# A new head for an interleaved attention and gMLP kernel: tokens, wq, wk, wv, with later background work queued behind its step

## The chip, the core and the metric

The kernel runs on one core of one Trainium2 chip. The metric is device time in microseconds (us), the median of several executions of the whole program. The core has a matrix engine (TensorE, PE in the profile), VectorE (DVE), ScalarE (ACT), GpSimd (POOL) and SyncE (SP), which here issues all transfers. Each engine runs its own instructions in order and waits for others by semaphores.

## What is computed

Four layers over x of 2048 tokens by 640: attention with a compressive memory, gMLP, the same attention again, the same gMLP again, with the same weights. Float32 results are kept by splitting each operand into a high and a low float16 part and summing three products. The reference, cut:

```python
def _A_ref(x, wq, wk, wv, wo, beta):            # H = 32 heads of Dh = 20, N = 4 segments of L = 512
    q, k, v = heads(x @ wq), heads(x @ wk), heads(x @ wv)
    for s in range(N):
        p = softmax(qs @ ks.T * scale + causal_mask)
        a_dot = p @ vs
        a_mem = (phi(qs) @ M) / (phi(qs) @ z + 1e-6)
        outs.append(g * a_mem + (1 - g) * a_dot)         # g = sigmoid(beta)
        M, z = M + phi(ks).T @ vs, z + sum(phi(ks))
    return concat(outs) @ wo
def _B_ref(x, w_in, w_sp, b_sp, w_out):
    z = gelu(x @ w_in)                                    # 2 x 864 columns
    g = w_sp @ layernorm(z[..., Fh:]) + b_sp[:, None]
    return (z[..., :Fh] * g) @ w_out
x = x + _A_ref(layernorm(x), ...)
x = x + _B_ref(layernorm(x), ...)
x = x + _A_ref(layernorm(x), ...)
x = x + _B_ref(layernorm(x), ...)
```

## The kernel before

Each of the two rounds has an attention phase (`phase1a`, class `Attention`), a phase with the output projection's rest and w_in (`phase1b`), and a phase with w_sp and w_out (`phase2`).

**Weights.** A weight is scaled by a power of two and split. `pow2_scales` finds the scale: largest magnitudes per partition, a PE transpose (tile `wtp`), a maximum over it (`wmx`), a diagonal (`wdg`), a PE product that spreads it to all partitions (`wbc`), and five small DVE steps to `pw` and its inverse `iv`. `split_scaled` makes the high part on ACT and the low part on DVE. `prologue` (L117) loads wv, wq and wk, in this order, five tiles of 128x640 each (`wst`), takes their maxima (`wamk`), scales and splits them, and computes small scalars. The maxima of wo, w_in and w_out come from `other_scales` (L168): 32 tiles `wmst` through a pool of two buffers, one DVE reduction each into `wap`, and one scale chain for all four.

**Attention.** A segment has 512 tokens, four tiles. `prep(t)` loads a tile of x, takes layernorm statistics (`lnst`), normalises, splits (high on ACT, low on POOL, tile `xnhl`) and transposes by a transfer into `xt`. `value(t)` makes v of a tile (`vps`), `unit(s, m)` one of five groups of 128 rows of q and k (`qps`, `kps`), which `out` splits (`qhl`, `khl`), stores to DRAM (`st`) and, for k, turns into features (`phl`, `pk`) for the memory update. In the first layer the head of the phase is: prep of tiles 0 to 3, values of 0 to 3, units 0 and 1. In the second layer `early` does this inside `phase2` of the round before.

**The loop.** `run` goes through 64 pairs of heads (16 in each segment), three steps for each pair, from step -10 (`LEAD`) on. A step issues scores: `mp` for the row maxima (`mx`, DVE) of the pair two ahead, `es` for this pair's exponentials (`P`, ACT, L865). Around them come casts (`PH` on ACT, `PL` on POOL), the products with v (`pv`), row maxima sent to the rows of `qk` (`mr`), and `fetch` of the next pair's q and k. Four streams are merged into it by due step, in `until`: `fills` (prep and loads for later values and projections, 11 and 3.5 steps ahead), `background` (`other_scales`, then load and split of wo and of half of w_in, paced in steps), `dense` (units, values and projections), `reads` (the memory's reads).

**Order.** The written order holds for PE alone. On the other engines and their queues the order is planned at build time by readiness and by priority, so an instruction that is ready early may be issued far ahead of where it is written. PSUM tiles `dn` (for `vps`, `qps`, `kps`) have two buffers, `mp` and `es` one each.

Of the kernel before, what the change touches and what calls it, by code (L numbers as in the profile page):

```python
# [47 lines left out]
def pow2_scales(g, pool, psum, tag, am, c0, n):  # L48

# [6 lines left out]
    nc.vector.tensor_scalar(dg[:n, :n], g.ident[:n, :n], mx[:n], None, ALU.mult)  # L56
    bc = psum.tile([128, 128], F32, tag=tag, name="wbc")
# [7 lines left out]
    nc.vector.tensor_scalar(iv, iv, WTOP, None, ALU.mult)  # L65


def split_scaled(g, h, l, st, c):

    nc = g.nc  # L70
    iv = g.iv[:st.shape[0], c:c + 1]
    nc.scalar.activation(h, st, AF.Identity, scale=iv)
    nc.vector.scalar_tensor_tensor(l, st, iv, h, ALU.mult, ALU.subtract)
# [43 lines left out]
def prologue(g, ctx, wv, wq, wk, wo, w_in, w_out):  # L117

    nc, tc = g.nc, g.tc
    wp = ctx.enter_context(tc.tile_pool(name="wqkv", bufs=1))  # L120
    g.w = {}
# [4 lines left out]
    nc.vector.memset(g.wap, 0.0)  # L126
    g.wam = wp.tile([128, 8], F32, name="wam")
    with tc.tile_pool(name="wpro", bufs=1, side="right", reuse_waits="tile") as p, \
            tc.tile_pool(name="wpp", bufs=1, space=PSUM, reuse_waits="tile") as pp:
        am = p.tile([128, 4, KD], F32, name="wamk")  # L130
        st = {}
        for i, (nm, dram) in enumerate((("v", wv), ("q", wq), ("k", wk))):
            st[nm] = p.tile([128, KD, D], F32, name="wst" + nm)
            for k in range(KD):
                nc.sync.dma_start(st[nm][:, k, :], dram[k * 128:(k + 1) * 128, :])
        for i, nm in enumerate("vqk"):
            for k in range(KD):
                nc.vector.tensor_reduce(am[:, i, k:k + 1], st[nm][:, k], AX.X, ALU.max, apply_absolute_value=True)
            nc.vector.tensor_reduce(g.wam[:, i:i + 1], am[:, i], AX.X, ALU.max)
            pow2_scales(g, p, pp, "wsc", g.wam, i, 1)  # L140
            h = wp.tile([128, KD, D], F16, name=f"w{nm}h")
            l = wp.tile([128, KD, D], F16, name=f"w{nm}l")
            for k in range(KD):
                split_scaled(g, h[:, k], l[:, k], st[nm][:, k], i)
            g.w[nm] = (h, l)

    pq, pk = g.pw[:, 1:2], g.pw[:, 2:3]
    s = lambda n: g.sc[:, n:n + 1]
    g.esc, g.rq, g.rk, g.gq, g.gk, g.sig, g.epsd, g.yw, g.zi, g.pofs = s(0), s(1), s(2), s(3), s(4), s(5), s(6), s(7), (s(8), s(9)), s(10)
    nc.vector.tensor_scalar(g.esc, pq, pk, SCALE / 16, ALU.mult, ALU.mult)  # L150
# [9 lines left out]
    nc.vector.tensor_scalar(g.rk, pk, 2.0 ** -24, None, ALU.mult)  # L160
    nc.vector.tensor_scalar(g.gq, g.iv[:, 1:2], XS, None, ALU.mult)
    nc.vector.tensor_scalar(g.gk, g.iv[:, 2:3], XS, None, ALU.mult)
    nc.vector.tensor_scalar(g.sig, pk, 1.0, 2.0 ** -20, ALU.min, ALU.mult)
# [4 lines left out]
def other_scales(g, stage, pool, psum, tag):  # L168
# [3 lines left out]
    for i, w in enumerate((g.wo, *g.wi, g.wu)):  # L172
        width = D if w.cols == D else w.cols // 2
        j = 0
        for k in range(w.nk):
            n = min(128, w.dram.shape[0] - 128 * k)
            for c in range(0, w.cols, width):
                t = stage.tile([128, D], F32, tag="bg", name="wmst")[:n, :width]
# [346 lines left out]
class Attention:  # L525
# [9 lines left out]
    def __init__(self, g, x, o_d, x1_d, kept):  # L535
# [11 lines left out]
        self.now, self.later, self.rd = None, {}, set()  # L547

    def post(self, k, f, free=False):
# [52 lines left out]

    def prep(self, t):
# [16 lines left out]
        return stats, norm  # L620

    def value(self, t):
# [5 lines left out]
        for n in range(2):  # L628
# [8 lines left out]
            def out(ps=ps.rearrange("p (h d) -> p h d", d=DH), v=self.vs[s % 2][:, t % 4, n * 16:(n + 1) * 16, :]):  # L637
                nc.scalar.mul(v[:, :, 0:DH], ps, QS)
                nc.vector.scalar_tensor_tensor(v[:, :, DH + 1:], ps, QS, v[:, :, 0:DH], ALU.mult, ALU.subtract)
# [39 lines left out]
    def unit(self, s, m):  # L679
# [3 lines left out]
        for nm in ("q", "k"):  # L683
            wh, wl = g.w[nm]
            ps = self.pd.tile([128, L], F32, tag="dn", name=f"{nm}ps")
# [118 lines left out]
    def fetch(self, n):  # L804
# [3 lines left out]
        for h in range(2):  # L808
            c = 40 * (n % 16) + 20 * h
            self.nc.sync.dma_start(self.qk[n % self.NQK][64 * h:64 * h + 60], self.st[n // 16 % 2][c:c + 20].rearrange("p l i c -> (p l) i c"))  # L810
# [19 lines left out]
    def scores(self, n, c):  # L830
# [30 lines left out]
        if 0 <= n < self.N:  # L861
# [3 lines left out]
            nc.scalar.activation(P[:, :, 512 * c:512 * c + ew], es[:, :, :ew], AF.Exp, scale=g.esc)  # L865
            if c == 2:
                self.last = n
        if 0 <= m < self.N:
            if c == 0:
                self.mx[m] = self.pl2.tile([128, 2, 4], F32, tag="mx", name="mx")  # L870
            for i, o, w in red:
                nc.vector.tensor_reduce(self.mx[m][:, :, i], mp[:, :, o:o + w], AX.X, ALU.max)  # L872
# [13 lines left out]
    def maxes(self, n):  # L886
# [7 lines left out]
        for i in range(2):  # L894
            nc.sync.dma_start(self.qk[n % self.NQK][60 + i:125 + i:64, 0].rearrange("h (t c) -> h t c", t=4), mr[:, i])
# [48 lines left out]
    def run(self, nseg=NSEG):  # L944
# [82 lines left out]
        def background():  # L1027

            g = self.g
# [10 lines left out]
        if self.stacked < 0:  # L1040
            for t in range(0, 4, 2):
                for f in zip(self.prep(t), self.prep(t + 1)):
                    f[0]()
                    f[1]()
                if t == 0:
                    self.start()
            for i in range(4, 8):
                self.early(i)
        else:
            self.start()  # L1050
# [109 lines left out]
```

## Time and profile before

| | |
|---|---|
| median of 3 runs | 2444.76 us (2442.37 to 2446.39) |
| profiled execution, its own time | 2440.32 us |
| its span, first to last instruction | 2438.6 us |
| mean granted TensorE clock | 0.975 |
| PE busy | 2218.2 us (91%) |
| DVE busy | 1434.3 us (59%) |
| ACT busy | 1133.7 us (46%) |
| POOL busy | 936.1 us (38%) |

The lines below are of that one execution. A timeline line gives the start in us from the span's start, the duration in us, the engine, the line of the kernel, the operation, the tile written and those read, and the count; in square brackets the time that the engine stood idle before it and what ended the wait. A line of a group gives count, busy us and mean ns, then idle time before its members and its releasers. A line of the stretches gives the length, each engine's busy us with its instructions, the granted clock, the share of the DMA engines and GB/s. Busy PE time is modelled and no measure of PE at its peak.

### The profile page before, as it was taken

Reading aid. Unit: us, or ns where it says so; the run is one execution under the profiler, and the core shown is the slowest. Engines: PE = TensorE matmul, PEld = TensorE weight load, DVE = VectorE, ACT = ScalarE, POOL = GpSimd, SP = SyncE. Lnnn points to the kernel's source line nnn. Section 1 sums busy time; section 2 is a strip of 40 time slices with the busy share of each in tenths; the row PEclk is TensorE's granted clock in tenths of the full one; section 3 lists DMA queues with packets and bytes.
Section 4 is the critical chain, followed back from the end, with each engine's and each line's share of the span. In section 5 each row is a group of like instructions: output and inputs, shape, how many; then the busy total and the mean of one; then the engine's idle time right before and its main releaser. Section 6 shows DMA issues by size and latency. Waiting matters only on the chain.

```text
span 2438.6 us, 50718 instructions
## 1 busy us (share of the span) xinstructions
PE 2218.2 (91%) x20682; PEld 1319.0 (54%) x20682; DVE 1434.3 (59%) x2766; ACT 1133.7 (46%) x1388; POOL 936.1 (38%) x728
## 2 busy tenths in 40 slices
PE   3698789999899989999997989999988997999998
PEld 2355455666555545555554556565654554555554
DVE  8668878777654555444326777877764452454441
ACT  3278777777632222212124988777762221121110
POOL 3168678888610100000002988887871010000000
PEclk9899999999999999999999999999998998999999
DMA  6824634344553488766445253443455345665762
GB/s 196 214 57 109 162 115 122 93 117 133 146 143 107 113 223 206 171 157 164 114 127 133 77 119 88 113 109 93 123 160 124 88 108 165 163 169 155 175 127 58
DMA packets 502505, 325.00 MB, mean 133 GB/s; under 512 B 408512, under 2 KB 443456, under 8 KB 497152
## 3 DMA queue, kind: packets, MB, share of 16 engines
q1 hardware_dynamic: 502272, 321.76, 51.4%
q8 instruction: 162, 2.65, 0.5%
q14 instruction: 71, 0.58, 0.1%
HBM read 148.25 MB, written 85.34 MB: 96 GB/s over the span
## 4 chain that ended last, share of the span: by engine, by line
PE 60%; DVE 11%; DMA 11%; ACT 7%; issue 5%; POOL 3%; SPq 3%; ACTq 0%; DVEq 0%; POOLq 0%
PE gp L380 16%; PE zp L295 14%; PE cyp L409 6%; PE pv L909 3%; PE yps L666 3%; PE kps L690 3%; DMA wr<-in_B_w_sp_dram 3%; PE vps L633 3%; PE mp L856 3%; PE qps L690 3%; ACT PH L882 2%; ACT P L865 2%; PE es L856 2%; POOL PL L883 2%; DVE mx L872 2%
## 5 line engine op out<-in xcount | busy, mean ns | idle before, releaser
L883 POOL TENSOR_TENSOR PL<-P,PH 128x1280 f16<-128x1280 f32 x248 | 649.8, 2621 | 155.2 <-ACT PH L882 145.6
L380 PE MATMUL gp<-zh,wt 128*128 128x432 f16 x2048 | 466.5, 348 | 24.0 <-DMA wt<-wn 24.0
L872 DVE TENSOR_REDUCE mx<-mp 128x2 f32<-128x1024 f32 (+3 forms) x512 | 409.4, 818 | 108.1 <-PE mp L828 106.2
L380 PEld LDWEIGHTS <-wt 128*128 128x128 f16 x3072 | 301.8, 98 | 286.5 <-DMA wt<-wn 25.7
L865 ACT ACTIVATE P<-es,sc 128x1024 f32<-128x1024 f32 (+1 forms) x384 | 370.3, 964 | 128.5 <-PE es L828 122.6
L882 ACT CAST PH<-P 128x1280 f16<-128x1280 f32 x256 | 320.5, 1253 | 19.0 <-PE pv L909 12.0
L295 PEld LDWEIGHTS <-th 128*128 128x128 f16 x1920 | 188.9, 99 | 177.8 <-issue 11.7
L380 PE MATMUL gp<-zl,wt 128*128 128x432 f16 x1024 | 272.8, 348 | 0.0
L395 POOL MEMSET un<- 128x64 f16 x32 | 4.8, 151 | 675.7 <-DMA ut<-un 588.9
L205 POOL TENSOR_TENSOR lnrs<-lnve,mhalf 128x1 f32<-128x1 f32 x96 | 58.6, 618 | 484.6 <-DVE lnve L204 459.6
L856 PEld LDWEIGHTS <-qk 60*128 60x128 f16 (+1 forms) x2048 | 93.0, 94 | 222.2 <-issue 155.1
L357 DVE TENSOR_REDUCE am<-wr 128x1 f32<-128x2048 f32 x32 | 73.2, 2286 | 214.7 <-DMA wr<-in_B_w_sp_dram 214.6
L383 ACT ACTIVATE u<-gp,bsp,un 128x864 f32<-128x864 f32 x32 | 34.2, 1068 | 355.5 <-PE gp L380 355.5
L409 PE MATMUL cyp<-wuh,ut 128*128 128x320 f16 (+1 forms) x896 | 166.8, 303 | 15.4 <-DMA ut<-un 15.4
L633 PE MATMUL vps<-wvh,xt 128*128 128x320 f16 x640 | 156.3, 310 | 22.5 <-DMA xt<-xnhl 13.8
L856 PE MATMUL es<-qk 64*128 64x512 f16 (+3 forms) x1024 | 135.2, 299 | 41.6 <-ACT P L865 26.9
L409 PEld LDWEIGHTS <-ut 128*128 128x128 f16 (+1 forms) x1344 | 132.6, 99 | 73.7 <-DMA ut<-un 17.4
L909 PE MATMUL pv<-vs,PL 128*128 128x41 f16 x2560 | 163.8, 181 | 7.3 <-POOL PL L883 4.5
L909 PE MATMUL pv<-vs,PH 128*128 128x41 f16 x2560 | 167.8, 182 | 1.2 <-DVE ab L925 1.2
L828 PEld LDWEIGHTS <-big 64*128 64x128 f16 x3072 | 141.7, 95 | 49.8 <-issue 3.1
L856 PE MATMUL mp<-qk 60*128 60x512 f16 (+3 forms) x1024 | 137.8, 306 | 31.1 <-DVE mx L872 28.6
L367 ACT ACTIVATE wn<-wr,ivw 128x1024 f16<-128x1024 f32 x64 | 71.9, 1144 | 194.6 <-DVE ivw L362 111.1
(182 smaller groups left out, 4138.5 us busy)
## 6 DMA issues: line engine op xcount, KB each, us to landing
wr<-in_B_w_sp_dram SPq DMA_DIRECT2D x32, 1024.0 KB
qk<-st SPq DMA_DIRECT2D x256, 120.0 KB
x<-x SPq DMA_DIRECT2D x56, 320.0 KB
z<-z SPq DMA_DIRECT2D x32, 432.0 KB
cz<-z SPq DMA_DIRECT2D x32, 432.0 KB
xt<-in_A_x_dram SPq DMA_DIRECT2D x32, 320.0 KB
st<-qhl SPq DMA_DIRECT2D x40, 256.0 KB
st<-khl SPq DMA_DIRECT2D x40, 256.0 KB
```

Source lines behind the costliest of these rows:

```text
L295: nc.tensor.matmul(zp[:, n, :FHH], a[:, k, :], b[:, k, c:c + FHH], start=(k == 0 and j == 0), stop=(k == KD - 1 and j == 2))
L380: nc.tensor.matmul(gp[:, n, :FHH], wt[:, k // 8, a, k % 8, :], b[:, k, n * FHH:(n + 1) * FHH], start=(k == 0 and j == 0), stop=(k == NT - ...
L409: nc.tensor.matmul(yp[:, n, :320], a[:kn[k], k, :], b[:kn[k], k, n * 320:(n + 1) * 320], start=(k == 0 and j == 0), stop=(k == KO - 1 and ...
L633: nc.tensor.matmul(ps, a[:, k, c], b[:, k, n * 320:(n + 1) * 320], start=(i == 0), stop=(i == 14))
L690: nc.tensor.matmul(ps, a[:, k, c], b[:, k, :], start=(i == 0), stop=(i == 14))
L828: nc.tensor.matmul(out, g.big[r, 64 - 64 * s:192 - 64 * s], mk, start=False, stop=s == 1, skip_group_check=True)
L856: nc.tensor.matmul(out[:, h, o:o + w], a[r, ac], b[r, bc], start=o == 0, stop=False, skip_group_check=True)
L865: nc.scalar.activation(P[:, :, 512 * c:512 * c + ew], es[:, :, :ew], AF.Exp, scale=g.esc)
L872: nc.vector.tensor_reduce(self.mx[m][:, :, i], mp[:, :, o:o + w], AX.X, ALU.max)
L882: nc.scalar.copy(PH, P[:, h])
L883: (nc.gpsimd if h == 0 or n < self.N - self.TAIL else nc.vector).tensor_tensor(PL, P[:, h], PH, ALU.subtract)
L909: nc.tensor.matmul(pv[:, i, h, :], x[:, c:c + 128], v[:, j, h0 + h, :], start=(j == 0 and x is PH), stop=(j == i and x is PL), skip_group_ ...
```

## The change

- `prologue` becomes `attn_weights` (tiles only) and `attn_scalars`; the work moves into `Attention.head`, which replaces the first layer's preps, values and early units. Loads: four tiles of x at once, wq, wk; wv is queued behind the four transposes of x. Then statistics of all four tiles, one power on POOL for all, four transposes; q's maxima, scale, splits; k's maxima queued behind q's second split; q of units 0 and 1; k's scale, splits; v's maxima behind k's second split; the scalars; k of units 0 and 1; v's scale and splits; the values. q and k of the head use the PSUM tiles of `es` and `mp`.
- `last_of` keeps the last traced exponential or value copy on ACT, row maximum or value copy on DVE, and fetch, maxima or weight transfer on SP. Under `hold()`, whatever is traced on these engines gets an order edge behind them: no wait for their end, only a later place in the queue. `until` runs `fills` and `background` under it, `prep` its statistics and norm, in both layers.
- `background` starts at step -8 and paces the 32 maxima at 0.75 step instead of from step 6 at 1.2. The scale chain is cut in two (`pow2_max`, `pow2_spread`), at steps 51 and 53, with the last maximum at 50. The transfer of b_sp moves behind it. The pools for wo and w_in are opened after the head.

```diff
+def pow2_max(g, pool, psum, tag, am, c0, n):      # pow2_scales up to wdg
+def pow2_spread(g, psum, tag, dg, c0, n):         # the rest of it
...
-    yield False
+    yield 50
     nc.vector.tensor_reduce(g.wam[:, 3:7], g.wap, AX.X, ALU.max)
-    pow2_scales(g, pool, psum, tag, g.wam, 3, 4)
+    yield 51
+    dg = pow2_max(g, pool, psum, tag, g.wam, 3, 4)
+    yield 53
+    pow2_spread(g, psum, tag, dg, 3, 4)
...
+    def hold(self):
+        held = ExitStack()
+        for i in self.last_of.values():
+            held.enter_context(self.tc.issue_after(i))
+        return held
...
+    def head(self):
...
+            for t in range(4):
+                nc.sync.dma_start(xs[:, t], self.x[t])
...
+            def largest(nm, behind):
+                a = p.tile([128, KD], F32, tag="wamk" + nm, name="wamk")
+                with tc.issue_after(behind):
+                    for k in range(KD):
+                        nc.vector.tensor_reduce(a[:, k:k + 1], st[nm][:, k], AX.X, ALU.max, apply_absolute_value=True)
+                i = WNAMES.index(nm)
+                return nc.vector.tensor_reduce(g.wam[:, i:i + 1], a, AX.X, ALU.max).ins
...
+            load("q")
+            load("k")
...
+            for t in range(4):
+                for i in range(2):
+                    nc.vector.bn_stats(sx[:, t, i, :], xs[:, t, i * 320:(i + 1) * 320])
+                nc.vector.bn_aggr(mv[:, t], sx[:, t])
+            nc.vector.tensor_scalar(rs, mv[:, :, 1], EPS, XS ** -2, ALU.add, ALU.mult)
+            nc.gpsimd.tensor_tensor(rs, rs, g.mhalf.to_broadcast((128, 4)), ALU.pow)
+            for t in range(4):
+                i = nc.vector.tensor_scalar(xs[:, t], xs[:, t], mv[:, t, 0:1], rs[:, t:t + 1], ALU.subtract, ALU.mult)
+                nc.scalar.copy(hl[:, t, 0], xs[:, t])
+            for t in (2, 0, 3, 1):
+                (nc.gpsimd if t > 1 else nc.vector).tensor_tensor(hl[:, t, 1], xs[:, t], hl[:, t, 0], ALU.subtract)
+            for t in (0, 1, 2, 3):
+                o = self.xt[0][:, :, :, t * 128:(t + 1) * 128]
+                last = nc.sync.dma_start(o.rearrange("p i k c -> p (i k) c"), hl[:, t].rearrange("p i c -> p (i c)"), transpose=True).ins
+            with tc.issue_after(last):
+                load("v")
+            qp = self.pe.tile([128, 2, 512], F32, tag="es", name="qp")
+            kp = self.px.tile([128, 2, 512], F32, tag="mp", name="kp")
+            largest("q", i.ins)
+            scale("q")
+            i = split("q")
+            largest("k", i[1])
+            units("q", 0, qp)
+            scale("k")
+            units("q", 1, qp)
+            i = split("k")
+            largest("v", i[1])
+            with tc.issue_after(i[-1]):
+                attn_scalars(g)
+            units("k", 0, kp)
+            scale("v")
+            units("k", 1, kp)
+            split("v")
+            for t in range(4):
+                for _ in self.value(t):
+                    pass
+                if t == 0:
+                    with self.hold():
+                        self.start()
...
-        return stats, norm
+        return lambda: held(stats), lambda: held(norm)
...
-            yield 6
+            yield -8
             if not g.wo.made:
-                for i, _ in enumerate(other_scales(g, self.bg, self.pl1, self.pm, "ms")):
-                    yield 6 + 1.2 * i if _ else 53
+                nc.vector.memset(g.wap, 0.0)
+                for i, _ in enumerate(other_scales(g, self, self.pl1, self.pm, "ms")):
+                    yield -8 + 0.75 * i if _ is True else _
+                nc.sync.dma_start(g.bsp, self.b_sp.rearrange("(t p) -> p t", p=128))
...
-                e[0] = next(e[2], None)
+                with self.hold() if e[1] < 2 else ExitStack():
+                    e[0] = next(e[2], None)
```

More of the change, by code (lines that the diff above doesn't have):

```diff
@@ L1040, in run @@
         if self.stacked < 0:
[L1041 to L1048, printed above, removed]
+            self.head()
         else:
             self.start()
+        g = self.g
+        g.top = [self.top.enter_context(g.tc.tile_pool(name=n, bufs=1, side="right", reuse_waits="tile")) for n in ("topi", "topo")][::-1]
         streams = [[next(it), i, it] for i, it in enumerate((fills(), background(), dense(), reads()))]
```

108 lines of the change are left out of this document (60 added, 48 removed).

## The prediction

> **What bounds the kernel now.** I read the table of stretches first, for where TensorE (PE) is not full; then VectorE's (DVE's) groups up to the first exponential; then the timeline of that stretch, and last the same landmarks in the second attention layer, which runs the same loop without a head.
>
> ```profile
> core 0: us, PE busy (x) PEld busy (x) DVE busy (x) ACT busy (x) POOL busy (x), PEclk, DMA share, GB/s
> 0.00:133.00 133.00, 73.73 (x408) 39.41 (x409) 95.17 (x216) 37.33 (x62) 27.05 (x48) 0.91 0.72 193
> 133.00:185.00 52.00, 46.92 (x738) 30.30 (x737) 37.61 (x74) 45.77 (x59) 41.24 (x23) 1.00 0.25 62
> ```
> ```profile
> 5.36 0.82 DVE L138 TENSOR_REDUCE wamk<-wstv 128x1 f32<-128x640 f32 x1
> ...
> 9.17 0.81 DVE L138 TENSOR_REDUCE wamk<-wstv 128x1 f32<-128x640 f32 x1
> ...
> 10.02 0.16 DVE L139 TENSOR_REDUCE wam<-wamk 128x1 f32<-128x5 f32 x1
> ...
> 15.18 0.14 DVE L65 TENSOR_SCALAR iv<-iv 128x1 f32<-128x1 f32 x1
> ...
> 32.78 1.46 SPq L219 DMA_TRANSPOSE xt<-xnhl  x1
> ...
> 36.33 0.45 PE L633 MATMUL vps<-wvh,xt 128*128 128x320 f16 x1 [9.19 <-DMA xt<-xnhl]
> ...
> 56.18 0.45 PE L633 MATMUL vps<-wvh,xt 128*128 128x320 f16 x1 [4.64 <-DMA xt<-xnhl]
> ...
> 67.23 0.59 PE L690 MATMUL qps<-xt,wqh 128*128 128x512 f16 x2
> ...
> 88.20 0.59 PE L690 MATMUL qps<-xt,wqh 128*128 128x512 f16 x2
> ...
> 110.75 1.01 PE L690 MATMUL kps<-xt,wkh 128*128 128x512 f16 x2 [9.52 <-DVE phl L724]
> ...
> 132.79 1.12 ACT L865 ACTIVATE P<-es,sc 128x1024 f32<-128x1024 f32 x1
> ...
> 184.77 1.11 ACT L865 ACTIVATE P<-es,sc 128x1024 f32<-128x1024 f32 x1
> ```
> PE does 73.7 us of work in the first 133 us. Its first real matmul comes at 36.3 because it waits for a transposed tile of x. The head (values of four tiles, q and k of units 0 and 1) ends where unit 2 of segment 0 begins, at 88.2. The first exponential of the loop, step 0, comes at 132.8, that of step 24 (pair 8) at 184.8: 2.17 us a step. From step 0 on the loop is dense: of the next 52 us ScalarE (ACT) works 45.8 and PE 46.9. So what a change of the head is worth is how much earlier step 0 comes, less what it pushes into the loop.
>
> In the head the busy engine is DVE, 95.2 of 133 us:
>
> ```profile
> L181 DVE TENSOR_REDUCE wap<-wmst 128x1 f32<-128x432 f32 (+1 forms) x31 | 20.4, 666 | 10.4 <-DMA wmst<-in_B_w_out_dram 7.9 <-DMA wmst<-in_B_w_in_dram 2.4
> L202 DVE BATCH_NORM_STATS2 lnst<-xt 128x6 f32<-128x320 f32 x20 | 8.8, 479 | 8.1 <-DMA xt<-in_A_x_dram 8.1
> ...
> L616 DVE TENSOR_SCALAR xt<-xt,lnmv,lnrs 128x640 f32<-128x640 f32 x10 | 6.1, 609 | 3.6 <-POOL lnrs L205 3.6
> ...
> L73 DVE SCALAR_TENSOR_TENSOR wkl<-wstk,iv,wkh 128x640 f16<-128x640 f32 x5 | 4.6, 951 | 0.0
> ...
> L138 DVE TENSOR_REDUCE wamk<-wstq 128x1 f32<-128x640 f32 x5 | 4.0, 804 | 0.0
> ```
> Two things here are not needed before step 0: the 31 maxima of the other weights (wap, 20.4 us) and the layernorms of six tiles of segment 1 and later (20 statistics stand for ten tiles, four are the head's). They sit between the steps that PE waits for.
>
> **The change, part by part.** *Loads.* x goes first, then wq, wk. Today's first tiles become usable between 5.36 and 9.17, four intervals, so 0.95 us per 320 KB. The four tiles of x are then there by 5.4 + 3 x 0.95 = 8.2, wq by 13.0, wk by 17.8. wv is queued behind the four transposes; it is used after 40, so this costs nothing unless it lands some 15 us late.
>
> *x.* After the last tile: two statistics (0.96), about 1.1 for aggregate, power and the waits between (an estimate, not a row of its own), four subtractions at 0.61: normalised at 12.7.
>
> ```profile
> L218 POOL TENSOR_TENSOR xnhl<-xt,xnhl 128x640 f16<-128x640 f32 x8 | 11.5, 1444 | 26.3 <-ACT xnhl L217 26.3
> ```
> Low parts of two tiles on POOL end near 13.4 + 2 x 1.44 = 16.3; a transpose is usable 3.55 us after its issue (32.78 to 36.33), so x is transposed by about 21. It is not what PE waits for: that is q.
>
> *The weights on DVE, one after the other.* Largest of q, 5 x 0.80, plus two low parts of x (at most 1.44 each, taken as 0.85): 18.4. The chain from the maximum to the scale took 5.2 us for wv (10.02 to 15.32) with other reductions between its steps; alone I take 4, bounds 3 and 5.2: 22.4. Splits, 5 x 0.95: 27.2. Then the largest of k (4.0), its chain (4), its splits (4.75): 39.9. The same for v: 52.7. PE's instructions are in written order, so it stands at each chain's transpose until the maximum is there; q0, q1, k0, k1 fit between. Head work on DVE that is not in this line (the halves of q and k, the key features, the scalars, some 9 us) mostly falls into the three chains' gaps; I add 2. The first value tile goes with the splits; for the other three, two tiles took 67.23 - 56.18 = 11.05 us today, 5.5 each: 54.7 + 16.5 = **71.2** for the end of the head against 88.2. Bounds: 64 (chains of 3, none of the other DVE work exposed, value tiles 0.8 shorter without today's waits between them, an estimate) and 82 (chains of 5.2, all 9 us of other DVE work exposed).
>
> [...]
>
> ```profile
> 40.00:60.00 20.00, 12.74 (x65) 7.63 (x64) 14.49 (x32) 6.98 (x13) 7.40 (x8) 0.83 0.61 157
> ```
> ```profile
> 83.69 1.01 PE L690 MATMUL kps<-xt,wkh 128*128 128x512 f16 x2 [6.58 <-DVE phl L724]
> ```
> After a wait of 6.58 us two matmuls took 1.01 us, against 0.59 at 88.20, and where PE waited often the granted clock was 0.83. Three islands with eight slow matmuls each, 0.21 us more apiece, are 5 us if all is exposed; I take nothing, since DVE paces q0 and k0, and keep the 5 inside the upper bound. [...]
>
> *From the end of the head to step 0.* Today 132.79 - 88.20 = 44.6. The second layer has no maxima here:
>
> ```profile
> 1280.52 0.60 PE L690 MATMUL qps<-xt,wqh 128*128 128x512 f16 x2
> ...
> 1297.80 1.01 PE L690 MATMUL kps<-xt,wkh 128*128 128x512 f16 x2 [7.77 <-DVE phl L724]
> ...
> 1322.32 1.12 ACT L865 ACTIVATE P<-es,sc 128x1024 f32<-128x1024 f32 x1
> ```
> It takes 41.8 there, with the same stall of unit 3's k on the features of the k before it. So this stretch hardly depends on the maxima: 43, bounds 39 and 47. Step 0 then comes at 114.2, **18.6 earlier** (bounds 4 and 30).
>
> *The maxima in the loop.* 32 of them at 0.75 step each from step -8: 11 fall before step 0, 21 x 0.67 = 14 us after. DVE is idle 52 - 37.6 = 14.4 us in the first 52 us of the loop, where ACT sets the pace. Free if all fit, 14 if none does; they sit between mp and its maximum, on a single buffer, so I take **5 lost**.
>
> *From step 51 on.*
>
> ```profile
> 251.01 1.11 ACT L865 ACTIVATE P<-es,sc 128x1024 f32<-128x1024 f32 x1 [0.88 <-PE es L828]
> ...
> 261.37 1.55 ACT L72 ACTIVATE woh<-wst,iv 128x640 f16<-128x640 f32 x2 [3.41 <-DVE iv L65]
> ...
> 266.00 0.83 ACT L72 ACTIVATE woh<-wst,iv 128x640 f16<-128x640 f32 x1 [2.47 <-DMA wst<-in_A_wo_dram]
> ...
> 268.32 1.09 ACT L865 ACTIVATE P<-es,sc 128x1024 f32<-128x1024 f32 x1
> ...
> 651.21 1.11 ACT L865 ACTIVATE P<-es,sc 128x1024 f32<-128x1024 f32 x1
> ```
> ```profile
> 1440.98 1.11 ACT L865 ACTIVATE P<-es,sc 128x1024 f32<-128x1024 f32 x1 [0.30 <-PE es L828]
> ...
> 1450.83 1.11 ACT L865 ACTIVATE P<-es,sc 128x1024 f32<-128x1024 f32 x1
> ...
> 1818.13 1.11 ACT L865 ACTIVATE P<-es,sc 128x1024 f32<-128x1024 f32 x1
> ```
> Pair 17 (of 64, counted from 0) takes 17.3 us in layer 0 and 9.85 in layer 1, because ACT, in order, stands at the split of wo, first for the scale, then for the load, with the next exponential behind it. From there to the last pair it is 400.2 against 377.2. The change spreads the chain over steps 50 to 53 and queues the splits of wo and w_in behind the step that they are paced for. Of the 7.5 of pair 17 between 0 and 7.5 goes, I take 4; of the other 15.5, which the splits themselves cost, between 5 lost (they move to steps where PE is fuller) and 8 won, I take 2: **6 won**.
>
> *Layer 1 and the rest.* Loads and norms of later tiles now queue behind the last transfer or reduction of their step. They have 11 steps of lead, a projection's load 3.5 steps (7.6 us), and a transpose is usable 3.55 us after its issue: nothing, give or take 4. On SP they stand behind the row maxima's transfers, which wait for ACT; who would wait is that projection. Splitting a function in two and moving b_sp cost nothing: b_sp is first read in phase 2.
>
> Sum: 18.6 - 5 + 6 = 20 us. The profiled execution took 2440.3 (span 2438.6), so it would take 2420; the median of the runs shown, 2444.8, lies 4.4 above it, so the forecast is **2425**.
>
> **The rivals.** *A. The loop waits for the loads of the maxima (slower).*
>
> ```profile
> 91.80 0.42 SPq L179 DMA_DIRECT2D wmst<-in_B_w_out_dram  x1
> ...
> 95.47 0.82 DVE L181 TENSOR_REDUCE wap<-wmst 128x1 f32<-128x640 f32 x1 [0.84 <-DMA wmst<-in_B_w_out_dram]
> ...
> 102.81 0.82 DVE L181 TENSOR_REDUCE wap<-wmst 128x1 f32<-128x640 f32 x1 [6.30 <-DMA wmst<-in_B_w_out_dram]
> ```
> A tile is usable 3.67 us after its issue and there are two buffers, so two tiles need 4.3 us, 2.2 each. The pace asks for one in 0.75 step, 1.6 us. If DVE meets the reduction at its step and not when the tile is there, it stands 0.6 us in each of 32, 19 us, with mp's maximum behind it, and the 14 us of work are exposed too: 18.6 + 6 - 19 - 14 = 8 slower, 2453. It decides once the wait per tile is over 0.33 us (18.6 + 6 - 14 = 10.6 us, over 32). For it: the wait of 6.30. Against: 31 tiles waited 10.4 us in all, and the order on DVE is planned from expected landings. *B. The head stays bound by DVE.* Without 21 maxima DVE has 95.2 - 14 = 81 us before step 0; if it keeps the 38 us of gaps it has now, step 0 comes at 119, 14 earlier, and with 8 lost in the loop and none won at step 51 the time is 2439. For it: the chains and the features still wait on one another; against: 18.5 us of those gaps (the 10.4 and the 8.1 of the rows above) are waits for loads that the change reorders or moves. *C. More is won.* The head ends at 64, the stretch after it takes 41, the maxima are hidden, and 12 of the 23 us that layer 0 is longer go: 28 + 12 = 40, 2405. For it: DVE's idle 14.4 against 14; against: it needs every term at its good end. That the edges do nothing (they only forbid an earlier issue) would leave the reordered head alone, and lies between B and the forecast.
>
> **How the numbers follow.** Forecast 0.55, A 0.12, B 0.18, C 0.15. The range 2405 to 2443 holds the forecast with its bounds, B, and the nearer half of C; A and the far half of C are left out. A measurement here tells 0.2%, 4.9 us, from no change: faster, 0.54 of the forecast's 0.55, half of B and all of C, 0.78; the same, the other half of B, 0.09; slower, A and the last hundredth, 0.13.
>
> **What would show it.** Right: the first unit matmul near 24 and not 36; unit 2 of segment 0 near 71; first exponential near 114; the eighth pair's about 15 earlier than today's; pair 17 near 13 us; PE waiting at three scale transposes. Wrong: the first exponential after 125, maxima of wap waiting tens of us for wmst with mp behind them, pairs 0 to 8 at 8 us and more, or projections that wait for o.

## The result, and the profile after

The changed kernel takes 2426.26 us (median of 4 runs, 2425.96 to 2432.53) against 2445.35 before (4 runs, 2442.37 to 2446.39): a ratio of 0.9931, 95% interval 0.9912 to 0.9949. The forecast was 2425.0. The time came out as forecast; two of the three terms of the sum did not, as the ledger shows. The profiled execution took 2432.5 us (span 2430.8).

| stretch, us | before | after | after, 2nd time | nohold | nomax | best3 |
|---|---|---|---|---|---|---|
| start to first exponential | 132.8 | 112.5 | 111.2 | 129.7 | 109.7 | 107.3 |
| pairs 0 to 7 | 52.0 | 66.9 | 65.0 | 52.0 | 53.9 | 64.0 |
| pairs 8 to 16 | 66.2 | 61.6 | 61.4 | 65.0 | 61.4 | 61.4 |
| pairs 17 to 30 | 138.5 | 137.7 | 140.1 | 139.9 | 134.8 | 135.0 |
| pair 31 to the last pair's first exponential | 261.7 | 261.5 | 261.2 | 264.7 | 264.2 | 262.0 |
| layer 1: end of round 1 to first exponential | 41.6 | 46.4 | 45.9 | 40.9 | 47.1 | 42.8 |
| layer 1: pairs 8 to 16 | 65.1 | 61.5 | 61.5 | 65.3 | 61.3 | 61.3 |
| layer 1: pairs 17 to 30 | 116.9 | 120.9 | 120.0 | 119.2 | 117.4 | 117.5 |
| layer 1: pair 31 to the last | 260.3 | 253.9 | 252.2 | 258.2 | 252.6 | 255.4 |

(nohold, nomax and best3 are experiments, below. Each column is one profiled execution. Not in the table, for before, after and the second time: layer 1's pairs 0 to 7, 53.5, 53.9 and 53.8; from the last pair of layer 0 to the end of round 1, 629.5, 629.9 and 630.2; and from the last pair of layer 1 to the end, 620.5, 624.0 and 624.9.)

The timeline of after, from the head to step 24. The columns are start, duration, engine, line, operation, and in brackets the idle time and its releaser:

```profile
10.21 2.18 DVE L658 TENSOR_SCALAR xs<-xs,mvx,rsx 128x640 f32<-128x640 f32 x4 [1.23 <-POOL rsx L656]
17.82 0.14 DVE L633 TENSOR_REDUCE wam<-wamk 128x1 f32<-128x5 f32 x1
20.39 0.15 DVE L75 TENSOR_SCALAR iv<-iv 128x1 f32<-128x1 f32 x1
23.13 1.01 PE L782 MATMUL qp<-xt,wqh 128*128 128x512 f16 x2 [3.56 <-DMA xt<-xhl]
...
40.46 0.39 PE L782 MATMUL kp<-xt,wkl 128*128 128x512 f16 x1 [3.15 <-DVE wkl L83]
...
45.84 0.58 PE L68 MATMUL wbc<-wdg,ones 1*128 1x1 f32 x2 [2.33 <-DVE wdg L60]
...
47.99 0.14 DVE L75 TENSOR_SCALAR iv<-iv 128x1 f32<-128x1 f32 x1
...
70.17 0.59 PE L782 MATMUL qps<-xt,wqh 128*128 128x512 f16 x2
...
112.46 1.12 ACT L957 ACTIVATE P<-es,sc 128x1024 f32<-128x1024 f32 x1
...
179.37 1.11 ACT L957 ACTIVATE P<-es,sc 128x1024 f32<-128x1024 f32 x1
```

The first unit's matmul comes at 23.1 (before, PE's first real matmul came at 36.3), unit 2 of segment 0 at 70.2 (88.2), step 0 at 112.5 (132.8), step 24 at 179.4 (184.8). So 20.3 us were won up to step 0, and 14.9 of them were given back in the next eight pairs. The table of stretches of after shows the same:

```profile
0.00:133.00 133.00, 88.05 (x604) 48.49 (x605) 93.64 (x208) 50.02 (x78) 28.73 (x44) 0.92 0.59 163
40.00:60.00 20.00, 15.40 (x76) 8.15 (x77) 15.20 (x41) 10.16 (x17) 0.00 (x0) 0.74 0.24 69
112.50:179.40 66.90, 51.73 (x739) 32.60 (x737) 52.06 (x100) 47.71 (x62) 44.95 (x26) 0.90 0.53 138
```

In the loop's first eight pairs PE's 51.7 us and ACT's 47.7 us now take 66.9 us, with DVE at 52.1 us of work (37.6 before).

### The profile page after: what moved, and what is told of

Read it like the earlier page. It is cut to its first block, busy times and chain, and to the rows that moved or that the text cites. A ratio compares the mean times of both kernels' runs of the same rounds, so it can differ in the third digit from the quotient of the medians.

```text
span 2430.8 us, 50694 instructions
## 1 busy us (share of the span) xinstructions
PE 2222.3 (91%) x20682; PEld 1322.2 (54%) x20682; DVE 1437.1 (59%) x2765; ACT 1133.3 (47%) x1388; POOL 934.0 (38%) x723
## 5 line engine op out<-in xcount | busy, mean ns | idle before, releaser
L964 DVE TENSOR_REDUCE mx<-mp 128x2 f32<-128x1024 f32 (+3 forms) x512 | 409.2, 817 | 109.7 <-PE mp L920 107.9
L948 PEld LDWEIGHTS <-qk 60*128 60x128 f16 (+1 forms) x2048 | 91.3, 94 | 225.0 <-issue 156.2
```

What stands on the lines that cost most here:

```text
L948: nc.tensor.matmul(out[:, h, o:o + w], a[r, ac], b[r, bc], start=o == 0, stop=False, skip_group_check=True)
L964: self.last_of["DVE"] = nc.vector.tensor_reduce(self.mx[m][:, :, i], mp[:, :, o:o + w], AX.X, ALU.max).ins
```

## Experiments

Each was timed in five rounds beside the kernel before. Its ratio is to that kernel, with a 95% interval.

**again.** The changed kernel once more. 

> The changed kernel once more, unaltered, for a second profile: in its first one the execution took 2432.5 us, its other three executions 2426. Ledger theory: the difference to the kernel before comes from five places, first exponential 20 us earlier, pairs 0 to 8 some 15 longer, pairs 8 to 17 some 4 shorter in both layers, layer 1's first exponential 5 later after the last product of the phase before, and the rest equal; then a second profile shows each of these again within 1.5 us and only one stretch that differs by about 6 us between a slower and a faster execution. Rival: the 15 us between pairs 0 and 8 are an accident of that one execution, then they fall below 9 here. Time 2426, ratio 0.992 to 0.993.

Measured: 2429.26 us, 0.9946 (0.9928 to 0.9963). It is the base for what follows, and its column of the ledger shows how far two profiles of one kernel differ: up to 2.4 us in a stretch. The longer pairs 0 to 7 came again (65.0), so they are no accident of one execution.

**nomax.** The loads and maxima of wo, w_in and w_out are left out, and their scales come from a constant:

```diff
-                nc.vector.memset(g.wap, 0.0)
+                nc.vector.memset(g.wap, 1.0)
...
-                t = a.bg.tile([128, D], F32, tag="bg", name="wmst")[:n, :width]
-                nc.sync.dma_start(t, w.dram[...])
...
-                    nc.vector.tensor_reduce(*last, AX.X, ALU.max, apply_absolute_value=True)
...
```

> Loads and maxima of wo, w_in and w_out are left out; their scales come from a constant, all else stays. Theory 1, the maxima cost the loop: pairs 0 to 8 take 52 to 54 us as in layer 1 and not 67, the first exponential comes 0 to 4 us earlier than 112.5 (11 maxima lie before it, mostly in waits), so the time is 13 to 19 us below the changed kernel, about 2410. Rival: the early loop is slow because norms of later tiles are now queued into it and it starts with PE half idle; then pairs 0 to 8 still take 60 us or more and the time falls by less than 8.

Measured: 2408.16 us, 0.986 (0.9837 to 0.9883). Pairs 0 to 7 take 53.9 us, so the maxima cost 11 to 13 us there. Stretches, DVE's groups and waits of after and then of nomax, over the same eight pairs:

```profile
L964 DVE TENSOR_REDUCE mx<-mp 128x2 f32<-128x1024 f32 (+3 forms) x33 | 26.6, 827 | 4.9 <-PE mp L920 4.7
L177 DVE TENSOR_REDUCE wap<-wmst 128x1 f32<-128x432 f32 (+1 forms) x20 | 13.2, 660 | 9.0 <-DMA wmst<-in_B_w_in_dram 5.1 <-DMA wmst<-in_B_w_out_dram 3.8
...
ACT P L957 <- PE es L920: 13.3, 13, 2.9
PE mp L948 <- DVE mx L964: 12.8, 9, 2.8
```
```profile
109.70:163.60 53.90, 46.85 (x739) 30.32 (x737) 41.27 (x79) 47.07 (x61) 44.54 (x26) 1.00 0.36 76
L949 DVE TENSOR_REDUCE mx<-mp 128x2 f32<-128x1024 f32 (+3 forms) x33 | 26.8, 829 | 9.9 <-PE mp L905 9.7
...
PE mp L933 <- DVE mx L949: 3.6, 6, 1.6
ACT P L942 <- PE es L905: 2.8, 5, 0.7
```

DVE is idle 53.9 - 41.3 = 12.6 us without the maxima and 66.9 - 52.1 = 14.8 with them. Its idle time did not shrink at all: the 10.8 us of added DVE work, and 2.2 us of added idle time, are the 13.0 us that the stretch grew. While DVE reduces a weight tile, the row maximum that PE's next `mp` waits for stands behind it (3.6 us of such waits became 12.8), and the exponentials behind that (2.8 became 13.3). PE's own work grew too: its 739 matmuls took 51.7 us at a granted clock of 0.90, against 46.9 at 1.00 without the maxima. No run here tells how much of the 13.0 us is that.

**pace.** One maximum in 1.4 steps:

```diff
-                    yield -8 + 0.75 * i if _ is True else _
+                    yield -8 + 1.4 * i if _ is True else _
```

> The maxima at 1.4 steps each instead of 0.75, so over steps -8 to 37. Theory 1a, waits for the loads: two buffers and 3.67 us from issue to use allow one tile in 2.2 us, the pace of 0.75 step (1.6 us) is under that and 1.4 steps (3.0 us) over it; the 9 us that DVE waited for tiles between pairs 0 and 8 go, and the 14 us of work spread into idle time: pairs 0 to 8 take 56 to 59 us, pairs 8 to 17 up to 3 more, time 6 to 10 us below the changed kernel, about 2418. Rival 1b, only the work counts: wherever a maximum falls it costs the loop its 0.67 us; then the loss moves to later pairs and the time stays within 3 us of 2426.

Measured: 2424.08 us, 0.9924 (0.9908 to 0.994). Pairs 0 to 7 take 59.1 us and pairs 8 to 16 68.4. Together that is 127.5 (128.5 in after, 126.4 the second time): the loss moved and did not shrink, as rival 1b had it. DVE still waits 11.5 us for tiles between pair 0 and pair 17.

**lag.** Four buffers, and each reduction three tiles behind its load:

```diff
-                if last is not None:
-                    nc.vector.tensor_reduce(*last, ...)
-                last = g.wap[:n, i, j:j + 1], t
+                if len(last) == 3:
+                    nc.vector.tensor_reduce(*last.pop(0), ...)
+                last.append((g.wap[:n, i, j:j + 1], t))
...
-        ... pool("abg", 2) ...
+        ... pool("abg", 4) ...
```

> Four buffers instead of two for the tiles of the maxima, and each reduction written three tiles after its load, so that a tile has some 5 us to land; pace 0.75 step as in the changed kernel. Theory 1a, DVE's waits for the tiles (9.8 us in all, 9 of them between pairs 0 and 8) are a loss of their own beside the 14 us of work: waits under 2 us, pairs 0 to 8 in 57 to 61 us instead of 65 to 67, time 5 to 9 us below the changed kernel. Rival 1b, the waits only fill time that the maxima's work takes from the loop anyway: waits gone, pairs 0 to 8 still 64 or more, time within 3 us of 2427.

Measured: 2425.59 us, 0.9934 (0.9919 to 0.9949). DVE's groups of lag over pairs 0 to 7:

```profile
L965 DVE TENSOR_REDUCE mx<-mp 128x2 f32<-128x1024 f32 (+3 forms) x33 | 26.7, 826 | 9.5 <-PE mp L921 9.5
L177 DVE TENSOR_REDUCE wap<-wmst 128x1 f32<-128x432 f32 (+1 forms) x20 | 12.4, 637 | 4.6 <-DMA wmst<-in_B_w_in_dram 3.4 <-DMA wmst<-in_B_w_out_dram 1.2
...
L182 DVE TENSOR_REDUCE wap<-wmst 128x1 f32<-128x640 f32 (+1 forms) x3 | 2.4, 812 | 0.5 <-DMA wmst<-in_B_w_out_dram 0.5
```

The waits for tiles fell from 9.0 to 5.1 us, yet the stretch takes 69.0 us (66.9), with 23 reductions in it instead of 21. The time went back into waits for `mp` (4.9 to 9.5). (The total says less: the four buffers make the rest of the first round 8 us longer, see best2.) So the waits for tiles are not the price. All kernels with maxima in the loop bear that out: their pairs 0 to 16 are longer than nomax's 115.3 us by 0.47 to 0.68 us for each reduction in them, near the 0.67 that one takes, and best2, whose 12 reductions there wait for no tile, pays 0.63. What is left is the reductions' own work. That their loads hold up the loop's own transfers does not show in the waits (PE's weight loads stood 0.8 us for rows of q and k in after, 0.2 in nomax), but no run keeps the loads and leaves out the reductions.

**nohold.** The order edges do nothing:

```diff
     def hold(self):
         held = ExitStack()
-        for i in self.last_of.values():
-            held.enter_context(self.tc.issue_after(i))
         return held
```

> The new head and the new pacing stay, but hold() puts no order edges on anything, so later loads, maxima, splits and norms go where they are ready. Theory: the edges win little by themselves. Layer 1, which has no new head, should return to its stretches of the kernel before (41.6 us from the last product of the phase before to its first exponential, 65 from pair 8 to 17, 117 from 17 to 31, 260 from 31 to the end), and in layer 0 maxima and later norms should go into the head's gaps and into the stretch up to the first exponential: that comes at 112 to 125, pairs 0 to 8 take 52 to 58; time 2418 to 2432. Rival: the edges are what lets the head be short, without them DVE takes the maxima between the chains as in the kernel before, the first exponential comes after 125 and the time is above 2435.

Measured: 2437.46 us, 0.9982 (0.9968 to 0.9995). The rival held: the first exponential falls back to 129.7, since DVE again takes the maxima before it:

```profile
L177 DVE TENSOR_REDUCE wap<-wmst 128x1 f32<-128x432 f32 (+1 forms) x31 | 20.8, 672 | 15.7 <-DMA wmst<-in_B_w_in_dram 9.2 <-DMA wmst<-in_B_w_out_dram 6.1 <-DMA wmst<-in_A_wo_dram 0.4
```

The reordered head alone wins 3 us up to step 0. The edges win 18 there, by pushing the maxima out, and cost 13 to 15 in the loop. The rest of their worth is in places that the prediction did not look at. The time from one pair's first exponential to the next's, summed over groups of pairs (us):

| pairs | before | nohold | after | chain53 | freebg |
|---|---|---|---|---|---|
| layer 0: 15 and 16 | 17.7 | 16.8 | 13.2 | 13.2 | 13.2 |
| layer 0: 17 | 17.3 | 14.8 | 17.0 | 13.8 | 17.0 |
| layer 0: 31 | 12.7 | 12.1 | 7.9 | 7.9 | 9.3 |
| layer 1: 15 and 16 | 17.0 | 17.0 | 13.2 | 13.2 | 13.2 |
| layer 1: 17 and 18 | 20.2 | 20.0 | 16.7 | 16.7 | 16.7 |
| layer 1: 19 to 21 | 23.2 | 24.1 | 33.3 | 29.5 | 29.8 |
| layer 1: 31 | 12.3 | 12.2 | 7.8 | 7.8 | 7.8 |
| layer 1: 46 and 47 | 18.6 | 16.6 | 15.1 | 15.1 | 15.1 |

With edges, pairs 15 to 18, 31, 46 and 47 are shorter and pairs 19 to 21 longer, in the layer without any maxima too. The timeline of before in layer 1, within pair 31, shows what the edges keep apart:

```profile
1558.35 0.49 DVE L202 BATCH_NORM_STATS2 lnst<-xt 128x6 f32<-128x320 f32 x1 [1.67 <-DMA xt<-x]
...
1561.98 2.61 POOL L883 TENSOR_TENSOR PL<-P,PH 128x1280 f16<-128x1280 f32 x1
1562.05 2.89 DVE L616 TENSOR_SCALAR xt<-xt,lnmv,lnrs 128x640 f32<-128x640 f32 x1
1563.10 1.11 ACT L865 ACTIVATE P<-es,sc 128x1024 f32<-128x1024 f32 x1 [2.43 <-PE es L828]
1564.86 1.28 DVE L872 TENSOR_REDUCE mx<-mp 128x2 f32<-128x768 f32 x2
```

DVE stands 1.67 us for a tile of x, and then 2.89 us in a norm that otherwise takes 0.61, with a row maximum behind it.

**normfree.** Statistics and norm are not held before step 0:

```diff
         def held(f):
-            with self.hold():
+            with ExitStack() if self.now is not None and self.now < 0 else self.hold():
                 f()
```

> Statistics and norms of prep lose their edge while the step is below 0, that is for tiles 4 and 5 of both layers; the loads keep theirs. Theory: in both layers PE waited for the transposed tile 4 (95.4 us and 1299.3 us in the profile of the changed kernel), whose norm stood on DVE behind the row maximum of step -5, 5.3 us in layer 1 and 6.6 in layer 0. Then layer 1's first exponential comes 4 to 5 us earlier after the last product before it (41.6 to 42.5 instead of 46.4), layer 0's 3 to 6 us earlier, the time is 6 to 11 us below the changed kernel, about 2418. Rival: the late thing is the load of tile 4, queued behind fetches; then both waits stay and the time is within 2 us.

Measured: 2420.66 us, 0.9905 (0.9887 to 0.9924). The first exponential comes at 106.6 (111.2), and layer 1 starts 1.6 us earlier (44.3 against 45.9). What the hold did at the start of layer 1, in the timeline of after:

```profile
1291.84 1.29 DVE L964 TENSOR_REDUCE mx<-mp 128x2 f32<-128x768 f32 x2 [3.52 <-PE mp L920]
1293.04 1.13 DVE L704 TENSOR_SCALAR xt<-xt,lnmv,lnrs 128x640 f32<-128x640 f32 x2
...
1295.90 1.34 SPq L218 DMA_TRANSPOSE xt<-xnhl  x1
...
1299.34 0.45 PE L725 MATMUL vps<-wvh,xt 128*128 128x320 f16 x1 [5.32 <-DMA xt<-xnhl]
```

DVE was free for 3.5 us, but the norm of two tiles was queued behind a row maximum that PE had not made ready. PE then stood 5.3 us for the transposed tile. Of the 4.8 us that layer 1 starts later than before, 2.7 remain without that hold, so the 4 to 5 us that were expected from it were too many, and the cause of the rest is open.

**chain53.** The scale chain in one piece at step 53:

```diff
-    yield 50
+    yield 53
...
-    yield 51
+    yield 53
```

> The scale chain of the four other weights is issued at step 53 as a whole again, instead of at 50, 51 and 53; all else as changed. Theory: the cut of the chain is worth next to nothing, since pair 17 takes 17 us with it as without (17.3 before, 17.0 after): pair 17 within 1.5 us of 17, time within 3 us of 2427. Rival, the cut saves the 4 us that the prediction gave it and something else took them back: pair 17 takes 20 to 22 us and the time is 2430 to 2433.

Measured: 2414.73 us, 0.99 (0.9883 to 0.9918). Pair 17 takes 13.8 us against 17.0. The timelines of after and then of chain53 from the chain's transpose on, with the exponentials of pair 17's later steps and pair 18's first:

```profile
243.76 0.27 PE L56 MATMUL wtp<-ident,wam 128*4 128x128 f32 x1 [2.26 <-DVE mr L985]
...
244.14 2.62 POOL L975 TENSOR_TENSOR PL<-P,PH 128x1280 f16<-128x1280 f32 x1
244.38 2.39 DVE L60 TENSOR_SCALAR wdg<-ident,wmx 4x4 f32<-4x4 f32 x1
245.60 1.11 ACT L957 ACTIVATE P<-es,sc 128x1024 f32<-128x1024 f32 x1
249.97 0.69 ACT L957 ACTIVATE P<-es,sc 128x512 f32<-128x512 f32 x1 [3.26 <-PE es L920]
...
252.16 2.60 POOL L975 TENSOR_TENSOR PL<-P,PH 128x1280 f16<-128x1280 f32 x1 [0.56 <-ACT PH L974]
...
252.27 2.52 DVE L189 TENSOR_SCALAR sc<-pw 128x2 f32<-128x2 f32 x1
...
254.70 0.16 DVE L75 TENSOR_SCALAR iv<-iv 128x4 f32<-128x4 f32 x1
...
257.96 1.12 ACT L957 ACTIVATE P<-es,sc 128x1024 f32<-128x1024 f32 x1 [5.88 <-PE es L920]
```
```profile
242.35 1.09 ACT L957 ACTIVATE P<-es,sc 128x1024 f32<-128x1024 f32 x1
...
243.90 0.69 ACT L957 ACTIVATE P<-es,sc 128x512 f32<-128x512 f32 x1 [0.46 <-PE es L920]
245.02 0.27 PE L56 MATMUL wtp<-ident,wam 128*4 128x128 f32 x1 [0.55 <-DVE wam L183]
...
245.92 0.22 DVE L60 TENSOR_SCALAR wdg<-ident,wmx 4x4 f32<-4x4 f32 x1
246.00 2.61 POOL L975 TENSOR_TENSOR PL<-P,PH 128x1280 f16<-128x1280 f32 x1 [1.23 <-ACT PH L974]
...
246.80 1.83 DVE L71 TENSOR_SCALAR pw<-pw 128x4 int32<-128x4 int32 x1
...
249.13 0.16 DVE L75 TENSOR_SCALAR iv<-iv 128x4 f32<-128x4 f32 x1
...
252.76 1.11 ACT L957 ACTIVATE P<-es,sc 128x1024 f32<-128x1024 f32 x1 [6.83 <-PE es L920]
```

The cut chain takes 11.1 us from transpose to `iv`, the whole one 4.3. The cut one met POOL's product `PL` twice: `wdg` and `sc`, steps of 0.2 us, began within it and lasted to its end. The whole one met it once (`pw`, 1.83 us). Cutting shortens the last wait of the pair (8.0 us from 249.97 to 257.96; before, 12.3) but lengthens the two steps ahead of it (9.0 us in after, 5.0 before and in chain53). So the pair stayed at 17. Neither expectation held: they had the pair at about 17, or at 20 to 22. The length of the chain does not decide the pair, though: over all kernels pair 17 takes 14.0 to 17.0 us with the cut chain (lag and best2 have 14) and 13.8 to 17.3 with the whole one.

**best2.** 16 of the 32 maxima in the head beside the value tiles, the others in the loop at 1.4 steps, with lag and normfree:

```diff
             for t in range(4):
                 for _ in self.value(t):
                     pass
...
+                for i in range(4):
+                    with self.hold():
+                        next(self.scales)
...
```

> From the results so far: half of the maxima (16) go into the head beside the four value tiles, where DVE has 9 us of work in 20, with four buffers and each reduction three tiles behind its load; the other 16 at 1.4 steps from step -8; statistics and norms without edge below step 0. Theory: pairs 0 to 8 fall to 54 to 58 us, the first exponential comes at 106 to 110, the rest of layer 0 as in the changed kernel; time 2408 to 2416. Rival: on DVE the value copies wait for the maxima's tiles and the values, which bound the head there, get longer; the first exponential comes at 113 or later and the time stays at 2418 or more.

Measured: 2418.23 us, 0.9904 (0.9888 to 0.992); first exponential at 110.2, pairs 0 to 7 in 61.6: the 54 to 58 us and the total of 2408 to 2416 that were expected did not come. Against normfree (106.6 and 68.3) that is 3.6 lost in the head for 6.7 won in the loop; lag and best2, with four buffers, are 6 to 8 us longer in the rest of the first round, where phase 1b starts later (its first product 19.4 and 19.7 us after the last pair's first exponential, 4.7 in after).

**freebg.** From step 54 on the background stream is not held:

```diff
-                with self.hold() if e[1] < 2 else ExitStack():
+                with self.hold() if e[1] == 0 or e[1] == 1 and t < 54 else ExitStack():
```

> One edit on the changed kernel: from step 54 on the background stream (copies of wo and w_in's half, and their splits) is no longer held behind its step; the maxima and the loads of x keep their edges. In layer 1 the kept copies of wo and w_in then load where they loaded before the change (1232 to 1250 us, ahead of the loop) and not at 1438 to 1445 us between the loop's own transfers. Theory (the held copies are what makes pairs 19 to 21 of layer 1 slow: 33.3 us in the changed kernel, 23.1 before): pairs 19 to 21 of layer 1 take 23 to 25 us, layer 0 stays within 3 us, total 2418 to 2423. Rival (pairs 19 to 21 are slow because of the held loads and norms of x, which this kernel keeps): they stay at 29 to 33 us and the total at 2426 to 2430.

Measured: 2423.49 us, 0.9936 (0.9924 to 0.9949). The kept copies of wo and w_in (the split weights that the first round stores for the second) do load early again (at 1222 to 1240 us), but pairs 19 to 21 of layer 1 take 29.8 us, not 23 to 25, and chain53, which leaves the copies within the loop, has 29.5. So this theory fell. Its rival's 29 to 33 us held, though not its total of 2426 to 2430. What is left as the reason for the longer pairs is the held loads and norms of x, which without edges stand in pairs 15 to 18; no run frees them alone, so this is not shown. Over pairs 15 to 21 of layer 1 it is 60.5 us before, 63.3 in after and 59.8 in freebg: moved, not saved.

**best3.** chain53 and normfree together. 

> Both edits that have won alone: the scale chain of wo, w_in and w_out in one piece at step 53 (2414.7 alone), and the norms of the head's and the layer's start not held (2420.7 alone). If their stretches are apart, as they lie (pairs 17 to 31; the first 112 us of layer 0 and the start of layer 1): 2429 - 14.5 - 6.5 = 2408, from 2404 to 2412, with the first exponential at 106 to 107 us and pair 17 at 13 to 14 us. Rival (the gain of the chain is a chance of where its small VectorE instructions meet GpSimd's 2.6 us products, which every shift of the schedule throws anew): pair 17 back at 15 to 17 us and the total at 2414 to 2421.

Measured: 2408.26 us, 0.9871 (0.9858 to 0.9885), the fastest kernel with all its work, 21 us below again by the medians and 18 by the ratios to the kernel before. The whole chain is worth 12.4 us on top of normfree and 14.5 on top of after by the medians, 8 and 11 by the ratios. But pair 17 takes 14.2 us (15.4 in normfree), pairs 17 to 30 as long as in normfree (135.0 against 135.1), and the rest of the gain lies in stretches without a chain. In best4 and best5, with the same chain, pair 17 is at 15.6 and 16.9. So the total followed the theory and the place did not: 1 to 3 us are shown to be pair 17, and why the rest comes with this edit stays open.

**best4.** best3 and freebg. 

> best3 and freebg together. If the copies are what makes pairs 19 to 21 of layer 1 slow there too (29.5 us in the kernel with the chain in one piece, 23.1 before the change): 6 us below best3, about 2402 (2397 to 2407). Rival (the copies cost the same wherever they go): equal to best3, 2406 to 2412.

Measured: 2410.97 us, 0.9883 (0.987 to 0.9897): no gain over best3. Freeing the background stream gave 4.5 us after pair 31 and took 5.7 in pairs 17 to 30.

**best5.** best4, with 16 maxima in the head and two buffers. 

> best4, and 16 of the 32 maxima in the head beside the value tiles, the other 16 in the loop at one in 1.4 steps; two buffers as in the changed kernel (so phase 1b starts as early as there). With four buffers this split gave a first exponential of 110.2 and 61.6 us to the eighth pair, together 3 us less than with all maxima in the loop (106.6 and 68.3). If that holds with two buffers: 3 us below best4, about 2399 (2394 to 2405). Rival (with two buffers VectorE waits for the tiles in the head as well, some 1 us for each pair of tiles): the first exponential at 114 or later and the total 3 to 6 us above best4.

Measured: 2415.59 us, 0.991 (0.9897 to 0.9924). First exponential at 113.9 (best4 107.0), pairs 0 to 7 in 58.7 (66.1): what the loop gains the head loses. The rival held.

## Why the prediction was right, point by point

**The head: right in size, with two waits misread.** Predicted and measured: x normalised 12.7 and 12.4; q's maximum 18.4 and 18.0; q's scale 22.4 and 20.5; splits of k done 39.9, and PE's wait for the last ended at 40.5; v's scale 47.9 (39.9 and twice 4) and 48.1; end of the head 71.2 and 70.2. DVE paced most of it, one weight behind the other. The chains were shorter than 4 us where nothing stood between their steps (2.7 for q; 3.9 for k) and longer for v (5.2, with 2.33 of PE waiting for `wdg`), and that evened out. Of PE's three waits at scale transposes one came, for q's maximum. At k's it was DVE that waited, for PE:

```profile
18.01 0.37 PE L56 MATMUL wtp<-ident,wam 128*1 128x128 f32 x1 [13.79 <-DVE wam L633]
...
29.05 0.15 DVE L633 TENSOR_REDUCE wam<-wamk 128x1 f32<-128x5 f32 x1
...
30.56 0.42 PE L56 MATMUL wtp<-ident,wam 128*1 128x128 f32 x1
...
31.02 0.28 DVE L58 TENSOR_REDUCE wmx<-wtp 1x1 f32<-1x128 f32 x1 [1.81 <-PE wtp L56]
```

Nor was the first unit held up by q alone: PE's wait before 23.13 ended with the transposed x, taken as there by 21 and "not what PE waits for".

The slow islands, stretches of PE's work between two waits, came. After a wait of 3.56 us two matmuls took 1.01 us at 23.13 (0.59 at 70.17), and the pairs still took 1.06 us up to 30.6, over 7.5 us with one wait of 0.89 in it. After a wait of 1.71 us the pairs took 1.01 and 1.06 us from 48.13 on, and 0.59 from 51.79 on. But after a wait of 3.15 us the pair at 40.69 took 0.59, and only the next, at 41.55, took 1.06. The granted clock was 0.74 between 40 and 60 us, and 1.00 between 20 and 40, where the first of these islands lies. So these rows show slow matmuls after some waits; what starts a slow stretch, and what ends it, is not shown. The islands were taken to cost nothing. But q's slow matmuls stood before k's transpose, so they had a part in the 1.81 us that DVE waited there. The head did not end the 5 us later that the prediction counts for all islands exposed (71.2 forecast, 70.2 measured); how much of the 5 us was hidden behind DVE and how much made up by other terms, no run tells.

**From there to step 0: right.** 43 predicted, 42.3 measured; step 0 came 20.3 earlier, 18.6 predicted.

**The maxima in the loop: wrong, 5 predicted, 13 to 15 measured.** The step that failed is "5 lost", between "free if all fit" and "14 if none does". DVE's 14.4 us of idle time before were counted as room. nomax shows that none of it was: with the maxima its idle time is 14.8. Most of DVE's gaps in before are short waits for `mp`, and a reduction of 0.66 us delays what ends them:

```profile
DVE mx L872 <- PE mp L828: 11.4, 12, 1.6
```

(waits in us, how many, the longest). Rival A's place was right, its mechanism was not: DVE stood 11.0 us for the 32 tiles in after and 9.9 the second time, 0.34 and 0.31 each, about the 0.33 from which A was to decide. But A's price of 33 us for waits and work did not come: both together cost 13 to 15. And lag took off nearly half of these waits in the eight pairs and gained nothing there.

**From step 51 on: wrong, 6 won predicted, none measured.** Pair 17 was to fall from 17.3 to 13; it took 17.0, since what the cut took from its last wait it added to the steps ahead. From pair 17 to the last pair of layer 0 it is 399.2 us in after (401.3 the second time) against 400.2.

**Layer 1: "nothing, give or take 4" held for the sum, out of larger parts of both signs.** Its attention is 0.8 us shorter in after, 4.0 in again. In after the start is 4.8 later (the held norm, in part), pairs 8 to 16 are 3.6 earlier, pairs 17 to 30 are 4.0 later, and from pair 31 on 6.4 earlier. The prediction looked only for who might wait for a delayed tile. It missed that tiles that land early also stand in DVE's way, as before's lines of pair 31 show.

**Rival B.** It was priced at 2439 with step 0 at 119. nohold came to 2437.5, with step 0 at 129.7 and a loop as fast as before. The line that edges doing nothing would lie "between B and the forecast" held for the total, if at its upper edge.

The sum of the terms was 20 us; the profiles show 7.8 (after) and 11.0 (again). Against the prediction, the maxima cost 8 to 10 us more and step 51 brought 5 to 7 less. The head brought 2 to 3 more, and pairs 8 to 16 of layer 0 another 4.6 that no term had. The phases behind layer 1's last pair took 3.5 and 4.4 us longer, which no term had either; the other changed kernels have 614 to 621 us there against 620.5 before, so its cause is open. The forecast met the median all the same: the profiled execution of after stands 6 us above its median and that of before 5 below. The second timing of the kernel, 0.9946, is some 13 us. So the way and the rough size of the change were right, and that the first median came within 1.3 us of the forecast is luck.

## What to carry to other kernels

An engine's idle time in a loop whose steps wait for one another need not be room for background work (here DVE's idle 12.6 us without the maxima became 14.8 with them): count each added instruction at its full price until a run without it says otherwise (in this loop, 0.47 to 0.68 us for a reduction of 0.67). Here 32 reductions cost 13 to 16 us up to pair 17 in the loop (237.6 and 241.0 us against 225.0 in nomax) and some 18 in the head (nohold's 246.7 less the 3.6 of its pairs 15 and 16, against the same 225.0; norms of later tiles move with the edges too), so a better place was worth little. Queueing background work behind its step paid here at pairs where early arrivals had collided with the loop (pair 31 of layer 1: 12.2 us in nohold, 7.8 in after), and cost where the step it waited for was itself late (PE stood 5.32 us for a transposed tile at the start of layer 1), so hold it by stretch and measure each stretch by itself.

## What the runs showed of the hardware

Some DVE instructions that begin while POOL runs its product `PL` (2.6 us) last until it ends, or a little longer. `wdg` took 2.39 us against 0.22, `sc` 2.52 against 0.16. The norm of a tile, in after:

```profile
L704 DVE TENSOR_SCALAR xt<-xt,lnmv,lnrs x28: 603/612/3006, 87.8 to 1612.6; 128x640 f32<-128x640 f32 x28
```

The three numbers are the shortest, the median and the longest in ns. Nine of these 28 began within a `PL` and took 1.81 us in the median (seven of them ended 0.35 us after it), the other 19 took 0.61. Not every instruction from SBUF to SBUF is held: in after the reciprocals `rs` took 0.20 us within a `PL` (104 of them) and outside (24), the reductions of 128x432 weight tiles 0.59 within (8) and 0.60 outside (12). Row maxima, which read PSUM, show nothing of it: at each of their four sizes the medians within and outside differ by at most 0.01 us. Why some are held and others not, no run here was made to tell.
